# Two attention blocks on one core: stack loads, x and weight pieces asked for at other places, the first maxima later, small VectorE work given more steps, and a new order of the main loop

## The chip, the cores and the metric

One core of a Trainium2 chip. The metric is the device time of one launch in microseconds (us), the median of several runs; lower is better. The engines are TensorE (PE, with its weight loads as PEld), VectorE (DVE), ScalarE (ACT), GpSimd (POOL) and SyncE (SP), which here issues nearly all DMAs, one after the other.

## The reference

Two independent attention blocks, A and B, each with its own x of 2048 rows by 640 columns, its own `wqkv` (640 x 1920) and `wo` (640 x 640), all float32, 32 heads of 20 columns:

```
qkv = x @ wqkv                        # q, k, v per head, Dh = 20, scale = Dh ** -0.5
A:  idx    = s - 2 * (0 .. 7)         # window of 8 keys, every second row back, masked below 0
    logits = sum_d q[s, d] * k[idx, d] * scale
    o      = softmax(logits over the 8) @ v[idx]
B:  scores = q @ k.T * scale          # all 2048 keys
    o      = softmax(scores) @ v
out = concat(A: o @ wo, B: o @ wo)    # 2048 x 1280
```

## The kernel before

Every float32 product is made exact enough by splitting an operand into a high and a low half (`split`: ScalarE casts the high half, VectorE or POOL subtracts to get the low half) and three passes over the pairs (`PASSES`). The output of a split is ready only when its raw piece has landed and both have run; `wait[0]` says how many ticks after the request these two are put into their engines' queues. A tick is one step of the program's own calendar (`tick`, `after(n, fn)`); it sets the order in which instructions are written, and each engine executes its own in that order.

The work comes in stages:

- q and k of A, 128 rows at a time, stored to DRAM (`qa_d`, `ka_d`). From there POOL computes A's whole attention in 16 tiles of 128 rows: each tile has 8 units (4 for scores, 4 for values), whose keys or values are fetched as rows (`akv`), multiplied and added in halves. `a_work` is a generator that writes POOL's next piece; `a_pace(us)` lets it write as much as POOL's own clock `gp.us` allows. A's softmax (`a_softmax`) has two small VectorE jobs per tile: a maximum (`am<-al`) and a reciprocal, put on a list (`soft_jobs`) with the number of steps until they are written.
- q and k of B: ten weight tiles (`w`), in five pairs `m = 0, 2 .. 8`, each with four column groups `n` and two weights `j`, so 8 groups a pair. The result is cast and its low half subtracted (`pr`), and stored to DRAM (`qb_d`, `kb_d`).
- v of A and then of B, in 15 "blocks" of four groups (`v_group`, `v_matmuls`; the sixteenth is finished later): block = 2 x (quarter of x) + half of the columns. x (`xn`, `xl`, loaded by `x_load`) and the weights (`ww`, loaded by `wide_pieces`, for B's v by `w_load`) come in pieces. POOL makes the low halves of x here, VectorE those of the weights. In each tick of most blocks `v_tick` also writes one step of B's maxima pass (`b_max`).
- B's main loop of 512 steps. B's heads are held in 8 "stacks" of four heads; a stack has k (`bk`), four chunks of q (`bq`) and v (`vb`), loaded by `b_pieces` and `v_piece` from DRAM. Each score is computed twice: once with the query rows as output rows for the maxima (VectorE, `mx<-ps_st`), which run `LEAD` = 52 steps ahead, and once with the keys as output rows for the exponentials (ScalarE, `e<-ps_st`) and the product with v (`b_pv`). Output parts are copied by ScalarE (`more`) and added by POOL (`braw<-braw,more`); `more` has four buffers, one taken every two steps. When a chunk is done, `normalize` sends its sums through DRAM (`s_d`), takes a reciprocal on VectorE (`sm<-sm`) and multiplies on POOL.
- In the main loop A's finished tiles are also turned: `a_turn` transposes in five parts on VectorE (`turn<-ao`) into a buffer of tag `stg` (three buffers, shared with `wo_a`'s pieces, loaded in `begin` from `loads` and split by POOL), sends them through DRAM and reads them back (`back`). Then TensorE multiplies them by `wo_a` (`out_chunk`).
- The last steps of B's loop and its output product.

The order of the main loop is written out in the string `ORDER`: `V` ends a step (product with v, and `begin` with its loads and jobs), `S` is two halves of scores with exponentials, `M` and `N` two halves of maxima, `Y` one of each, `j` a part of a turn, `H` a part of A's output product; the digits are PSUM banks. It was made by a planner outside of the kernel; the kernel only reads it.

All DMAs of SP stand in one queue order. The DMA semaphores go round over eight places, so a DMA is issued only when the one eight places before it has landed.

In the listing the functions print as they were. In the profile almost all instructions have line 70 (71 after the change), that of the helper which issues them, so tiles are told apart by their names.

Of the kernel before, what the change touches and what calls it, by code (L numbers as in the profile page):

```python
# [74 lines left out]
def attention_pair(ctx, tc, xa, wqk_a, wv_a, wo_a, xb, wqk_b, wv_b, wo_b, oa, ob):  # L75
# [327 lines left out]
    def a_attention():  # L403
# [3 lines left out]
        for n, (t, c) in enumerate(UNITS):  # L407
# [3 lines left out]
            run_jobs(soft_jobs, 2)  # L411
# [335 lines left out]
    def b_pv(i):  # L747
# [159 lines left out]
    def v_tick(us, maxima=True):  # L907
# [4 lines left out]
        if q_loads:  # L912
            for _ in range(4):
                q_loads.pop(0)()
# [11 lines left out]
    def w_load(half):  # L926

        WV[1][half], pieces = wide_pieces(wv_b[half])
        wait[0] = 2
# [3 lines left out]
    x_load(1, 5)  # L933
    for block in range(15):
        c, half = divmod(block, 2)
        s0 = c % 4 * 4
        if block in (0, 14):
            for s in range(s0, s0 + 4):
                v_group(c, half, s)
                v_tick(2.2, False)  # L940
        else:
            ps4 = [bank() for _ in range(4)]
            for second in range(2):
                for u in range(2):
# [5 lines left out]
                    v_tick(V_US)  # L950
        if half:
            if c < 6:
                x_load(c + 2, 3)
# [4 lines left out]
        if block in (6, 7):  # L958
            w_load(block - 6)
# [28 lines left out]
    def begin(i):  # L988

        g, sub = divmod(i, NQC * NKB)  # L990
        if sub == (1 if g else 2) and g + 1 < NG:
            k_loads, q_loads = b_pieces(g + 1) if g else ([], q1_loads)
            for n, fn in enumerate(k_loads + q_loads + [lambda g=g + 1: v_piece(g, 0, NKB)]):
                after(1 + (n // 2 if n < 8 else 2 * n - 12), fn)
# [3 lines left out]
        if loads and i % 2:  # L998
# [5 lines left out]
        if done_a and done_a[0][0] <= 0 and len(turned) + len(turn_jobs) < 2:  # L1004
# [13 lines left out]
        "Y07M1S36Y54V0Y71S26M4Y03V7Y06M4S31Y72V0Y13M4S76VY71M2S64Y05V7Y64S31N02VY06S15M3Y27V6Y01M3S52VY70M1S53Y46V0Y75"  # L1018
        "M1S34VjS73jM5S42Y10jV7jM5S43Y02VS16M4S30Y27jV1Y36M4S07VY26S03M4Y71V6S02jM4Y37VY02S13M4S76Y02jV1jS75jM3Y26VY07"
        "Y53M1S46Y70V3Y45M1jS67VY04M5S71Y23V0Y17M5S42VY71M3S25S06N17V2Y03S14M5VY70M3S15S26Y07V1M3S27Y65VM3S07Y25V6jY01j"  # L1020
        "S73jH54jH54S02H54Y71H54Y03H54M1VjY70M4S31Y26V0Y73M4S12VY71H62N35S04H62Y71H62Y03H62Y54H62M0Y73V5Y46M0S72VS74M2"
        "S60N15V7S64M2Y01VM5S04Y32V7Y01M5S43VY04H32Y15Y76H32Y40H32Y15H32Y47H32M0S65V4Y73S62M0VY73S26M0V5Y74S32M0VN74S36"
        "H01Y25H01Y73H01Y46Y25H01H01M3Y76V2M0S73Y45VY07S16M3V5Y70S12M3VY07S61M3V2Y07S65M3VY07M5S41H32H32Y70H32Y14Y56H32"
        "Y70H32S14M5V7Y03S21Y64VM2S01Y45V6Y70M2S15VY70S15M2Y46V0Y71M2S54VY71M4S63Y20V1Y76S53N42VS07N63H45M1H45S06H45Y73"
        "H45H45M1S06Y73V4Y50M1S36VY07S35M1Y64V7Y03S21N56VY05M2S14Y67V5Y01S42N36VY70S14M2Y65V0Y71M2S46VjS71jM4S63Y20V7j"
        "M4S61Y30VY61S25Y43jN07jS61V2Y03S45N67VY06M3S51Y72V6Y50M3S17VY05S71M3S26N50V7Y14M2S65VY06M4S13Y72Y60V1Y75M3S26V"
        "Y07M5Y24S31Y70V2Y13M5S74VY70M3S15S26N70V1S25M3Y76VY02S73M4S61N02V7S63M4Y01VY62S03S45N17V6S03M1Y74VY05H12Y73H12"
        "Y64Y05H12Y37H12Y64H12Y03Y75V6Y41M2S05VY70S15Y42N36V7S05N12S34VN06S51Y23V4Y05M6S13VY05S13M6Y24V5Y01S67N32VY06M3"
        "S71H25H25Y06H25Y71Y34H25Y06H25Y71N34V0S17S62N35VM3S71Y56V2jY70M3S16VjY70S15M3S62jY07V1jM3S56Y72VM3S05Y26V7S01"
        "S35jN64VM0S26Y34V5Y70M1S64VS07Y63S42N15V0Y73S16N45VY71M2S46S50N17V4Y35M1S06VY07M5S31S42N70V3Y41M5S72VY70M1S46"  # L1030
        "S35N07V4Y36M1S05VY07M5S31S42N70V3S41M5Y72VY04M5S71Y23V0Y17S64Y52VY71Y62H34H34Y50H34Y72Y61H34Y05H34S72N61V0Y36"
        "S75N14VY71M2S65Y40V1Y76M2S54VY07M5S42Y31V7Y04S65M2VS06M4S13Y27V0M4S16Y73VY12H65Y74H65Y03H65Y41Y72H65Y03H65Y41"
        "N72V0S13M5Y74VY31S72Y65N04V3S72Y15Y06VjM4S72Y61V0jS75jM3Y12VY75M3S61S20jY75jV6M3S21Y05VM3Y72S15V0Y74S16M2VY71"
        "S64M2Y50V1S76M2Y45VY07S62M3S51N07V6S52M3Y01VY75S04M2S16V7Y05M2S14VY06S51M2S47N06V5S41M2Y07VY64S03M1S75N64V0S71"
        "M2Y65VY71S62M3S50N71V6S52M3Y70VY51Y72H34Y06H34S51H34Y27H34Y05H34M6S21V0Y35M6S42VY15S24M6Y30V5Y12M6S43VY04M1S37"
        "Y65V4Y03M1S76VY07M5S31Y24V7Y03M5S12VY04M1S35Y67V4Y03S52N16VS70Y15H23N46H23S75H23Y40H23Y17H23M5S04N71V2S03M5S74"
        "VM0S73Y65V4jY70M1S35VjY07S63Y52Y14jV7jM2S06Y45jVM2S01Y65V4Y70M2S51VY07S16M2S54N70V1Y23M5S74VS07M2S46N51V0S72M3"
        "Y56VY71S25M3S60N71V2S36M4Y70VY13S74M5S02N13V7S06M4Y12VY06S15M3S27N06V1S25M3Y07VS26S05M3Y71V2Y03S46N15VY70M3H16"
        "S25H16Y07H16Y24Y53H16H16N70S24Y53V1Y02M6S34VS02M3S75Y61V0M3S72Y15VM3S72Y56V1Y07M3S26VY07S62Y35Y41V7M5S02Y13VM5"
        "S04Y32V1Y07M5S24VY07Y23H45Y61H45S07M2H45Y61H45Y07H45M2S61V0Y74S56Y13VM4S73Y62V1jY07S54M2VS07jM5S42Y31V0jM5S74"  # L1040
        "Y21VN73S46S52Y10Y74jV3jM5S40Y21VM5S70Y41V2Y37M5S01VS70M3S15Y62V7M3S01Y25VM3S06Y51V2Y07M3S16VY70M5S41S32N07V4"
        "Y35S06M1VY07M5S31S42N70V3Y41M5S72VY70M1S46S35N07V4Y36M1S05VY07M5S31S42V7Y03S61M4VS06Y32H14N57H14S02H14Y56H14"
        "Y07H14M2Y56V7Y04M2S15VS06M4S13Y27V0M4S16Y73VM4S61Y23V7Y06S15M3VY06M1S35Y47V6Y03M1S54VY70S53M1H46H46Y70H46Y53"
        "Y21H46Y70H46M2S51V7Y06S54M2VY06S15M2Y47V6Y01M2S54VjS70jM4S13Y26V7jY01M4S63VM0S26Y54jV3jY70M1S46VY07S64M1S35N70"
        "V6Y14S32Y75VY01M3S25V7Y60M1S34VY06S53M1S47N60V5Y41M2S67VY04M6S13S25N40V1Y27S63M4VY07M2S64S51N70V6Y52M3S71VY70"
        "M1S53S46N07V5Y41M2S06VY70S61M2S45N07V6S41Y23N05VY74S03H21N56H21S74H21Y05H21Y37H21M4S06V7Y13S02M4VY06S13M4Y27V6"
        "M0S53Y42VM0S75Y43V2Y75M0S64VY73M5S40Y12V7Y03M5S41VM3S02H15Y67H15Y04Y23H15Y67H15Y04H15M2S76V0Y15S74M2VY71S64M2"
        "S50V1Y76M2S45VjY07S64M2V5jY70S61M2VjY07S61M2S45jY70jV6M2S41Y05VY74M2S15V0Y74S16M2VY71S64Y53M0S72Y63V4Y57S01M2V"
# [3 lines left out]
        "S75Y46V1jY07M2S56VjY07M5S42S31jY70V4Y35S62M0VY73S65M0V2Y73S46M0VY73S46M0Y52V7Y63M0S45VY62M3S50S71Y26M3S05Y76V1"
        "Y02S34M5VY07S23M5Y41V7Y02M5S34VS03M1S46Y57V0Y14M2S76VY15S74M2V6Y50S71M2VY70S15M2Y46V0Y71M2S54VN71S64H52Y03H52"
        "S67H52Y41H52Y30H52N71Y64V0Y75S16M2VY71M4S63Y20V1Y76M4S32VY07M2S64Y51V7Y06M2S45VY06M4S13Y27V6Y01M4S32VY70Y13H24"
        "Y56H24S70N13H24S56H24Y71H24N03Y56V1Y07S24N35VY07S62M3Y51V7S06jM3S25VjM0S26Y34V5jS70jM1Y64VY70M1S36Y45jV0S76M1"
# [121 lines left out]
```

## Time and profile before

| what | value |
|---|---|
| median of 3 runs | 1779.23 us (1778.9 to 1779.62) |
| profiled execution | 1781.89 us, of which the span is 1780.1 |
| mean granted TensorE clock | 0.988 of full speed |
| busy in the span, TensorE | 1734.6 us, 97% |
| VectorE, ScalarE, POOL busy | 1358.2, 1340.4, 1265.4 us |
| TensorE idle for VectorE's maxima (`mx`) | 24.1 us in 12 waits, longest 8.7 |
| TensorE idle for `bq` from DRAM | 11.3 us in 2 waits, longest 11.0 |

How to read it: times run from the start of the span. TensorE is busy nearly throughout, and the other engines work beside it, so the stretches in which it stands still are few, and the timeline shows each with its start and the instruction that released it. q and k of A end at about 147 us, q and k of B at about 283, the v stage at about 470, A's work on POOL at about 1410. Shares of busy time are averages over these stages. The clock has to be read by windows: it is 1.0 in most of them.

### The profile page before, as it was taken

What the parts mean: (1) busy time and instruction counts of PE and PEld (TensorE: products, weight loads), DVE (VectorE), ACT (ScalarE), POOL (GpSimd) and SP (SyncE); (2) the same over time, 40 slices, a digit from 0 to 9 for tenths busy, and PEclk for the clock granted to TensorE, in tenths of its full rate; (3) what the DMA queues carried; (4) which work ended last, traced back from release to release, by engine and by line L of the source; (5) the groups of instructions that cost most, each with busy time, mean ns of one, the idle gap of its engine ahead of it and who ended that gap; (6) DMA issues with size and microseconds to landing.
All of it is one profiled execution on the core that took longest, in us unless ns stands there. A gap on an engine that the chain in (4) does not pass through costs nothing. (4 is left out here: it accounts for less than half of the span.)

```text
span 1780.1 us, 34705 instructions
## 1 busy us (share of the span) xinstructions
PE 1734.6 (97%) x12711; PEld 1014.8 (57%) x12711; DVE 1358.2 (76%) x1814; ACT 1340.4 (75%) x2658; POOL 1265.4 (71%) x1119
## 2 busy tenths in 40 slices
PE   9999997989979999999999999999999999999999
PEld 8988876989735544444444444344434455444569
DVE  3113332888679999999999999899989999999400
ACT  4223222222479999999999999899989999999981
POOL 0001941698889999999999999999998943545242
PEclk9999998999999999999999999999999999999999
DMA  6447868565764345335436533643552432111123
GB/s 221 122 148 256 273 216 257 194 224 174 218 172 128 99 128 165 114 116 159 131 101 176 148 104 107 186 122 102 167 156 85 115 102 52 40 32 55 33 70 114
DMA packets 194435, 248.29 MB, mean 139 GB/s; under 512 B 89308, under 2 KB 114396, under 8 KB 193272
## 3 DMA queue, kind: packets, MB, share of 16 engines
q1 hardware_dynamic: 193688, 245.41, 45.7%
q8 instruction: 100, 1.64, 0.4%
q14 instruction: 71, 0.58, 0.1%
q10 hardware_dynamic: 576, 0.66, 0.1%
HBM read 181.08 MB, written 64.91 MB: 138 GB/s over the span
## 5 line engine op out<-in xcount | busy, mean ns | idle before, releaser
L70 DVE TENSOR_REDUCE mx<-ps_st 128x1 f32<-128x512 f32 (+1 forms) x1490 | 1226.5, 881 | 74.6 <-PE ps_st L70 63.2
L70 ACT ACTIVATE e<-ps_st 128x512 f32<-128x512 f32 x2048 | 1066.5, 626 | 49.4 <-PE ps_st L70 35.4
L70 PE MATMUL ps_st<-bk,bq 60*128 60x512 f32 x2048 | 563.4, 439 | 31.1 <-DVE mx L70 19.2
L70 PE MATMUL ps_st<-e,vb 128*32 128x512 f32 x4096 | 546.6, 608 | 5.7 <-DVE mx L70 4.9
L70 PE MATMUL ps_st<-bq,bk 62*128 62x512 f32 x2048 | 549.9, 433 | 0.9 <-ACT e L70 0.6
L70 PEld LDWEIGHTS ps_st<-bq,bk 62*128 62x128 f32 x2048 | 274.6, 185 | 407.8 <-ACT e L70 260.1
L70 POOL TENSOR_TENSOR braw<-braw,more 128x512 f32<-128x512 f32 x224 | 288.1, 1286 | 108.3 <-ACT more L70 107.8
L70 PEld LDWEIGHTS ps_st<-bk,bq 60*128 60x128 f32 x2048 | 258.9, 185 | 128.9 <-DVE mx L70 72.8
L70 POOL TENSOR_TENSOR akv<-akv,aq 128x1280 f32<-128x1280 f32 x64 | 188.5, 2945 | 166.7 <-DMA akv<-ka_d 166.7
L70 POOL TENSOR_TENSOR akv<-akv 128x640 f32<-128x640 f32 (+3 forms) x304 | 283.4, 932 | 15.0
L70 ACT COPY ro<-ps_st 128x320 f32<-128x320 f32 (+2 forms) x172 | 73.6, 465 | 176.9 <-PE ps_st L70 112.1
L70 PE MATMUL ps_st<-ww,xn 64*128 64x320 f32 (+1 forms) x1776 | 189.9, 313 | 0.8 <-DVE ww L70 0.6
L70 PEld LDWEIGHTS ps_st<-ww,xn 64*128 64x128 f32 (+1 forms) x1776 | 178.3, 190 | 16.3 <-ACT e L70 8.3
L70 PEld LDWEIGHTS ps_st<-e,vb 128*32 128x32 f32 x4096 | 82.3, 108 | 155.6 <-issue 76.1
L70 POOL TENSOR_TENSOR akv<-akv,al 128x1280 f32<-128x1280 f32 x64 | 151.5, 2367 | 0.6 <-ACT e L70 0.6
L70 ACT COPY more<-ps_st 128x512 f32<-128x512 f32 x224 | 135.7, 606 | 5.3 <-PE ps_st L70 4.6
L70 PE MATMUL ps_st<-xn,w 128*128 128x512 f32 x480 | 116.4, 390 | 1.9 <-DVE w L70 1.9
L70 POOL TENSOR_TENSOR xn<-stg,xn 128x512 fp32r<-128x512 f32 (+1 forms) x30 | 53.8, 1805 | 81.8 <-ACT xn L70 80.5
L70 PEld LDWEIGHTS ps_st<-xn,w 128*128 128x128 f32 x480 | 90.0, 188 | 22.0 <-DVE w L70 2.8
L70 PE MATMUL ps_st<-ww,aot 64*128 64x320 f32 x960 | 100.3, 308 | 0.0
L70 PEld LDWEIGHTS ps_st<-ww,aot 64*128 64x128 f32 x960 | 91.7, 186 | 4.9 <-issue 0.7
L70 ACT CAST pr<-ps_st 128x512 fp32r<-128x512 f32 x40 | 23.5, 586 | 93.4 <-PE ps_st L70 90.5
(65 smaller groups left out, 1045.2 us busy)
## 6 DMA issues: line engine op xcount, KB each, us to landing
akv<-ka_d SPq DMA_DIRECT2D x128, 320.0 KB
akv<-va_d SPq DMA_DIRECT2D x128, 320.0 KB
kb_d<-pr SPq DMA_DIRECT2D x20, 512.0 KB
qb_d<-pr SPq DMA_DIRECT2D x20, 512.0 KB
bk<-kb_d SPq DMA_DIRECT2D x16, 640.0 KB
bq<-qb_d SPq DMA_DIRECT2D x64, 160.0 KB
stg<-xb SPq DMA_DIRECT2D x16, 512.0 KB
rb<-s_d SPq DMA_DIRECT2D x128, 64.0 KB
```

Of the source, the lines that this page charges most:

```text
L70: return self.tc.keep_in_program_order(op(*a, **k))
```

## The change

Eight edits and a new `ORDER`:

- While B's q and k are made, A's pace on POOL is reckoned with groups that are 0.91 as long (`A_SLOW`).
- In the last pair (`m == 8`) the stack of heads 0 to 3 is asked for from the third to the sixth group, its first chunk of q after the seventh, x of the first quarter after the second; the first weights of v in the seventh group of the pair before; the second weights after the last group.
- x of the second quarter is asked for after the second group of the first block, not ahead of it; x of later quarters is split at the fourth tick after its request, not the third.
- The first two blocks have no maxima; they start with the third. The queries of stack 0 are then asked for two DMAs a tick instead of four.
- The weights of B's v are asked for after block 4 (split nine ticks later) and within block 7 (split four ticks later), instead of after blocks 6 and 7 (two ticks later).
- A's small softmax jobs have 5 steps instead of 3, with one more piece of POOL's calendar behind each; the general run of two jobs ahead of each unit goes.
- The reciprocal of B's sums is taken 8 steps after the sums were sent instead of 6.
- In the main loop, loads of the next stack come one a step, `wo_a`'s pieces one in each of the first steps, and turning starts only when no `wo_a` piece is left and after step 10.

```diff
+A_SLOW = 0.91
...
-        job(soft_jobs, 3, lambda: dve.tensor_reduce(m[:, 0], L.rearrange("p o h -> p h o"), AX.X, ALU.max))
+        job(soft_jobs, 5, lambda: dve.tensor_reduce(m[:, 0], L.rearrange("p o h -> p h o"), AX.X, ALU.max))
         yield
+        yield
+        run_jobs(soft_jobs, 9)
...
-        job(soft_jobs, 3, lambda: dve.reciprocal(m[:, 0], m[:, 0]))
+        job(soft_jobs, 5, lambda: dve.reciprocal(m[:, 0], m[:, 0]))
         yield
+        yield
+        run_jobs(soft_jobs, 9)
...
             a_fetch(n + 2)
-            run_jobs(soft_jobs, 2)
...
-                elif m == 8 and (n, j) == (0, 1):
+                elif m == 6 and (n, j) == (3, 0):
                     w0, loads = wide_pieces(wv_a[0])
-                elif m == 8 and n == 3:
-                    if j == 0:
-                        wait[0] = 4
+                elif m == 8:
+                    g8 = 2 * n + j
+                    if g8 == 1:
+                        k_loads, q_loads = b_pieces(0)
+                        wait[0] = 5
+                        XV = [x_pieces(xa, 0)]
+                        for fn in XV[0][1]:
+                            fn()
+                    elif 1 < g8 < 6:
+                        k_loads.pop(0)()
+                    elif g8 == 6:
+                        for _ in range(4):
+                            q_loads.pop(0)()
+                    elif g8 == 7:
+                        wait[0] = 3
                         w1, more = wide_pieces(wv_a[1])
                         for fn in more:
                             fn()
-                if m == 8 and (n, j) == (1, 1):
-                    wait[0] = 3
-                    XV = [x_pieces(xa, 0)]
-                    for fn in XV[0][1]:
-                        fn()
-                    wait[0] = 2
-                if m == 8 and n > 1:
-                    if (n, j) == (2, 0):
-                        k_loads, q_loads = b_pieces(0)
-                    k_loads.pop(0)()
...
-                    a_pace(QK_US * groups)
+                    a_pace(A_SLOW * QK_US * groups)
...
-            normalize(raws.pop(u), g, qc * 512, *((2, 3) if last else (5, 6)), (lambda: out_last(qc)) if last else None)
+            normalize(raws.pop(u), g, qc * 512, *((2, 3) if last else (5, 8)), (lambda: out_last(qc)) if last else None)
...
-        if q_loads:
-            for _ in range(4):
-                q_loads.pop(0)()
+        for _ in range(min(2, len(q_loads))):
+            q_loads.pop(0)()
...
-    x_load(1, 5)
...
-        if block in (0, 14):
+        if block < 2:
             for s in range(s0, s0 + 4):
                 v_group(c, half, s)
                 v_tick(2.2, False)
+                if (block, s) == (0, 1):
+                    x_load(1, 5)
...
+                if block == 7 and not second and u:
+                    w_load(1, 4)
+        if block == 4:
+            w_load(0, 9)
         if half:
             if c < 6:
-                x_load(c + 2, 3)
+                x_load(c + 2, 4)
...
-        if block in (6, 7):
-            w_load(block - 6)
...
-                after(1 + (n // 2 if n < 8 else 2 * n - 12), fn)
+                after(1 + (n if n < 8 else 2 * n - 7), fn)
...
-        if loads and i % 2:
+        if loads and (i % 2 or i < 12):
             loads.pop(0)()
...
-        if done_a and done_a[0][0] <= 0 and len(turned) + len(turn_jobs) < 2:
+        if done_a and done_a[0][0] <= 0 and len(turned) + len(turn_jobs) < 2 and not loads and i > 10:
             a_turn(*done_a.pop(0)[1:])
...
-        "Y07M1S36Y54V0Y71S26M4Y03V7Y06M4S31Y72V0Y13M4S76VY71M2S64Y05V7Y64S31N02VY06S15M3Y27V6Y01M3S52VY70M1S53Y46V0Y75"
...
+        "Y07S61M2Y45V0Y71S26M3Y05V7Y06M3S52Y71V0Y26M3S75VY71M5S24S03N17V2Y06S15Y34VM0S74Y56V3Y70S21N46VY70M4S12S63N07V1"
...
```

How the edits move instructions is seen in each engine's own order. First VectorE in the third and fourth pair of B's q and k, before: `w` is the low half of a weight tile, `pr` that of a result, `am<-al` the maximum of one tile of A.

```order
L70 TENSOR_TENSOR w<-stg,w 128x640
L70 TENSOR_REDUCE am<-al 128x32
L70 TENSOR_TENSOR pr<-ps_st,pr 128x512
L70 TENSOR_TENSOR w<-stg,w 128x640
L70 TENSOR_TENSOR pr<-ps_st,pr 128x512 x7
```

The same place now:

```order
L71 TENSOR_TENSOR w<-stg,w 128x640
L71 TENSOR_TENSOR pr<-ps_st,pr 128x512
L71 TENSOR_TENSOR w<-stg,w 128x640
L71 TENSOR_REDUCE am<-al 128x32
L71 TENSOR_TENSOR pr<-ps_st,pr 128x512 x7
```

The maximum has moved from ahead of the second weight's low half to behind it.

SP at the end of B's q and k and the start of the v stage, before (`wv_a` weights of A's v, `bk` and `bq` keys and queries of stack 0, `xa` x of A, `va_d` rows of v):

```order
L70 DMA stg<-wv_a 128x640 x2
L70 DMA stg<-wv_a 128x320
L70 DMA bk<-kb_d 40x4096
L70 DMA qb_d<-pr 128x2x512
L70 DMA bk<-kb_d 22x4096
L70 DMA stg<-xa 128x2x512 x2
L70 DMA stg<-xa 128x512
L70 DMA va_d<-ro 128x320
L70 DMA bq<-qb_d 20x1024
L70 DMA bq<-qb_d 40x1024
```

And now, from the third piece of k on:

```order
L71 DMA bk<-kb_d 40x4096
L71 DMA qb_d<-pr 128x2x512
L71 DMA bk<-kb_d 22x4096
L71 DMA qb_d<-pr 128x2x512
L71 DMA bq<-qb_d 20x1024
L71 DMA bq<-qb_d 40x1024
L71 DMA bq<-qb_d 20x1024
L71 DMA bq<-qb_d 40x1024
L71 DMA qb_d<-pr 128x2x512
L71 DMA stg<-wv_a 128x640 x2
L71 DMA stg<-wv_a 128x320
L71 DMA va_d<-ro 128x320
```

k and the first queries of stack 0 have moved ahead of the last store of q, and the second weights of v, which stood ahead of the last pieces of k, now stand behind all of them.

VectorE in the first steps of the main loop, before (`turn<-ao` are parts of a turn, `mx<-ps_st` maxima of scores):

```order
L70 STREAM_TRANSPOSE turn<-ao 128x128 x2
L70 TENSOR_REDUCE mx_4423<-ps_st 128x2
L70 TENSOR_REDUCE mx_4423<-ps_st 128x1
L70 STREAM_TRANSPOSE turn<-ao 128x128 x2
L70 TENSOR_REDUCE mx_4423<-ps_st 128x2
L70 TENSOR_REDUCE mx_4423<-ps_st 128x1
L70 TENSOR_REDUCE am<-al 128x32
```

And now:

```order
L71 TENSOR_REDUCE mx_2158<-mx_4500 128x16
L71 STREAM_TRANSPOSE mtr<-mx_2158 128x32
L71 TENSOR_REDUCE mx_5061<-ps_st 128x2
L71 TENSOR_REDUCE mx_5061<-ps_st 128x1
L71 STREAM_TRANSPOSE turn<-ao 128x128 x2
L71 TENSOR_REDUCE mx_5061<-ps_st 128x2
L71 TENSOR_REDUCE mx_5061<-ps_st 128x1
```

The first turn has moved from ahead of the end of a set of maxima (`mx_2158<-mx_4500` gathers it) to behind it.

More of the change, by code (lines that the diff above doesn't have):

```diff
@@ L924, in x_load, with w_load @@
             fn()
-    def w_load(half):
+    def w_load(half, w):
         WV[1][half], pieces = wide_pieces(wv_b[half])
-        wait[0] = 2
+        wait[0] = w
         for fn in pieces:
             fn()
-    x_load(1, 5)
     for block in range(15):
@@ L1022, in attention_pair @@
[L1022 to L1036, printed above, removed]
@@ L1052, in attention_pair @@
[L1052 to L1055, printed above, removed]
-        "Y34VY75S61M2Y40V7Y61S25M3VY06M1S53S74Y60M1S35Y70V4Y36M1S05VY07S63M1Y54V7Y60S13N25VY06S14M2Y57V6Y01M2S45VY70M4"
@@ new lines, in attention_pair @@
+        "Y06H35M1Y74V0Y35M1S76VY73M4S62Y10V3Y76M4S21VY07M1S64Y53V7S60M1Y45VY06Y14H32Y75H32Y06H32Y14H32Y07H32M5Y41V0S72"
+        "M3Y56VY71S25M3Y60V7Y15M3S62VY06M1S53Y74V6S50N13Y27VY05Y41H23Y76H23Y05H23Y41H23Y07H23M4S61V0VY71M4S63H20H20Y17"
+        "H20Y36Y54H20Y17H20M5Y34V1S07M2Y65VY07S62M3Y51V0Y72S63M4VY71M2S64Y05V1Y74S26N30VN72S36H54Y01H54Y73H54Y62Y01H54"
+        "H54M6Y32V0Y15M6S43VY15M3S27Y06V5Y12S74N30VY76S41M2Y05V6Y74M2S10VY75H01Y24H01Y35Y76H01Y24H01Y35H01M6Y24V3S05M1"
+        "S76VjM4S70Y12V6jY75M3S02VY70S15M3S26jY07V1jM3S25Y76VjM3S02Y56V7Y04S31N26VY05S14M2Y67V5Y01S42N36VY70S14S32N65"
@@ new lines, in attention_pair @@
+        "jY46V7S05S12M3VM5Y01S43V2Y07M5S14VY70M3H56S21H56Y70H56N24S31H56Y70H56M2Y14V7S06Y51N23VS04M5S12Y73V0Y16M4S32V"
+        "Y71S63M4V2Y70S16M4VY70Y16H54M2H54S70H54Y61H54H54M2S07N16V5S04M2Y71VS04M6Y32V1Y04M6S53VY02M4S37Y61V2Y03S74M5V"
+        "Y70M3S15H62H62Y70H62N15S34H62Y70H62Y13N45V7S60M2Y14VS05M2S16Y74V0Y15M2S46VY71S54M2V6Y70S51M2VY70S15M2Y46V0Y71"
+        "M2S54VY71M4H63S02H63Y71H63N04S52H63Y71H63N05Y24V7S60M2S15VY06S14M2V5Y06S71M2VY07S64M2S15N70V6Y14M2S75VY70M4S13"
+        "S26N07V1Y25M3S06VY07Y62S53Y41N70V6S51S23N74VM0S72Y54V3Y07S61N24VY07M5S12Y43V7Y01S62N54VY06S51M2S47N60V5Y41M2"
@@ L1078, in attention_pair @@
+        "Y07M5S31S42N70V3Y41M5S72VY70M1S46S35N07V4Y36M1S05VY07M5S31S42N70V3Y41M5S72VY70M1M5S43S70")
     owed = []
```

87 lines of the change are left out of this document (48 added, 39 removed).

## The prediction

> **What bounds the kernel now.** I read the page's busy shares first, then TensorE's (PE's) waits, then the timeline at each long wait, then the clock around it. Busy shares and span:
>
> ```profile
> span 1780.1 us, 34705 instructions
> PE 1734.6 (97%) x12711; PEld 1014.8 (57%) x12711; DVE 1358.2 (76%) x1814; ACT 1340.4 (75%) x2658; POOL 1265.4 (71%) x1119
> ```
>
> TensorE is idle for 1780.1 - 1734.6 = 45.5 us. The change leaves the arithmetic as it is, so it can act only on that idle time and on what idling costs in clock. Who ends TensorE's waits (us in total, times, longest):
>
> ```profile
> PE ps_st L70 <- DVE mx L70: 24.1, 12, 8.7
> PE ps_st L70 <- DMA bq<-qb_d: 11.3, 2, 11.0
> PE ps_st L70 <- DVE w L70: 1.9, 2, 1.4
> ...
> PE ps_st L70 <- DVE ww L70: 0.6, 2, 0.3
> ```
>
> So 38 of the 45.5 us sit in a few places. The timeline of TensorE (start, duration, instruction, in brackets the idle time before it and its releaser) has them:
>
> ```profile
> 232.20 2.58 PE L70 MATMUL ps_st<-xn,w 128*128 128x512 f32 x10 [1.38 <-DVE w L70]
> 306.98 0.76 PE L70 MATMUL ps_st<-bk,bq 60*128 60x512 f32 x1 [11.00 <-DMA bq<-qb_d]
> 387.41 0.79 PE L70 MATMUL ps_st<-bk,bq 60*128 60x512 f32 x2 [4.32 <-DVE mx L70]
> 506.99 0.80 PE L70 MATMUL ps_st<-bk,bq 60*128 60x512 f32 x2 [8.71 <-DVE mx L70]
> 827.52 1.06 PE L70 MATMUL ps_st<-e,vb 128*32 128x512 f32 x8 [0.85 <-DVE mx L70]
> 1132.13 1.93 PE L70 MATMUL ps_st<-e,vb 128*32 128x512 f32 x8 [3.90 <-DVE mx L70]
> 1330.60 1.22 PE L70 MATMUL ps_st<-bk,bq 60*128 60x512 f32 x3 [3.42 <-DVE mx L70]
> ```
>
> Behind each of the five waits of 3.42 us or more the windows show the granted clock at half (the number ahead of the DMA share), and none behind 0.85:
>
> ```profile
> 298.70:312.00 13.30, 4.75 (x29) 4.24 (x31) 2.36 (x2) 2.71 (x3) 8.11 (x5) 0.50 0.67 223
> 387.50:394.20 6.70, 6.36 (x40) 5.58 (x42) 3.65 (x4) 0.00 (x0) 6.31 (x7) 0.50 0.92 304
> 503.60:510.30 6.70, 3.31 (x14) 1.03 (x14) 4.84 (x9) 1.57 (x3) 6.25 (x6) 0.51 0.50 153
> 827.00:833.00 6.00, 5.47 (x40) 2.12 (x42) 5.93 (x8) 5.04 (x11) 6.00 (x6) 1.00 0.61 172
> 1131.70:1138.30 6.60, 6.17 (x26) 2.00 (x28) 4.41 (x8) 2.20 (x5) 6.60 (x5) 0.50 1.00 300
> 1329.70:1336.30 6.60, 5.70 (x23) 2.06 (x27) 4.53 (x6) 3.10 (x6) 6.52 (x5) 0.50 0.61 202
> ```
>
> Work done at half clock takes twice as long, so each long wait costs half of its window's PE time more: 2.4, 3.2, 1.7, 3.1 and 2.9 us. That is an upper bound, as some of that time is not bound by the clock.
>
> **The change part by part.** VectorE's (DVE's) side of the stalls, and the POOL and SP rows that matter:
>
> ```profile
> 199.55 0.63 DVE L70 TENSOR_REDUCE am<-al 128x32 f32<-128x256 f32 x1 [4.58 <-POOL al L70]
> 200.70 2.42 DVE L70 TENSOR_TENSOR w<-stg,w 128x640 fp32r<-128x640 f32 x1
> 380.24 5.98 DVE L70 TENSOR_TENSOR ww<-stg,ww 128x640 fp32r<-128x640 f32 x3
> 398.98 1.95 DVE L70 TENSOR_TENSOR ww<-stg,ww 128x640 fp32r<-128x640 f32 x3
> 505.31 0.51 DVE L70 STREAM_TRANSPOSE turn<-ao 128x128 f32<-128x128 f32 x2 [8.87 <-POOL ww L70]
> 1131.28 0.25 DVE L70 RECIPROCAL sm<-sm 128x16 f32<-128x16 f32 x1 [3.85 <-DMA sm<-s_d]
> 1328.82 0.59 DVE L70 TENSOR_REDUCE am<-al 128x32 f32<-128x256 f32 x1 [3.92 <-POOL al L70]
> ...
> 281.70 3.53 SPq L70 DMA_DIRECT2D stg<-wv_a  x3
> 293.90 7.97 SPq L70 DMA_DIRECT2D bq<-qb_d  x4
> 342.20 1.45 SPq L70 DMA_DIRECT2D stg<-xa  x3
> 363.67 2.43 SPq L70 DMA_DIRECT2D stg<-xb  x3
> ...
> 291.61 0.73 ACT L70 CAST ww<-stg 128x640 fp32r<-128x640 f32 x1 [3.39 <-DMA stg<-wv_a]
> 292.39 0.56 PE L70 MATMUL ps_st<-ww,xn 64*128 64x320 f32 x4 [0.23 <-ACT ww L70]
> 302.77 1.04 ACT L70 CAST xn<-stg 128x1024 fp32r<-128x1024 f32 x1 [7.80 <-DMA stg<-xa]
> 303.89 4.65 POOL L70 TENSOR_TENSOR xn<-stg,xn 128x1024 fp32r<-128x1024 f32 x2 [59.91 <-ACT xn L70]
> 356.01 1.29 POOL L70 TENSOR_TENSOR xl<-stg,xl 128x512 fp32r<-128x512 f32 x1
> 400.91 2.38 POOL L70 TENSOR_TENSOR xn<-stg,xn 128x1024 fp32r<-128x1024 f32 x1 [2.75 <-ACT xn L70]
> ```
>
> *Slower pacing of A in the q/k stage (A_SLOW).* At 199.55 the softmax maximum of A stands in VectorE's row ahead of the low half of a weight (200.70) and holds it for 4.58 us. The order of the changed kernel has it behind that low half. The two waits on `w`, 1.9 us, shrink to what the 2.42 us low half costs by itself: 0.7 left, gain 1.2. What of A's work is not done here comes later on POOL, which idles in the v stage (59.91 us ahead of 303.89): nothing.
>
> *Stack 0 and the first maxima.* Now 11.00 idle, 2.4 of clock and 0.6 on `ww`: 14.0. The four bq issues take 7.97 us because the queue is full of large bk transfers. In the new order bk and the first bq are asked for some groups earlier, and the maxima start at the third block, so the 11.00 goes. Two things are late next. First, the weights of v's second block are asked for behind them, after the last q store. Their first cast came 291.61 - 281.70 = 9.9 us after the first issue, and TensorE needed them about 292. Asked for at 286 to 290 (four groups of bk in front) they are there between 290 and 299: a stall of 0 to 8, I take 5, plus 2 of clock (1.7 to 3.2 after the others). Second, x of the second quarter: its casts now stand behind the block's second copy, so they begin one group before its use. Cast 1.04 and low halves 4.65 and about 1.3 end 7 after they begin, 3.4 beyond what a group and the queue behind it hide. New cost 5 + 2 + 3.4 = 10.4, gain 3.6 (bounds: none of it late 14.0; both at their worst and the clock twice, 8 + 3.2 + 3.4 + 2.4 = 17, a loss of 3).
>
> *The weights of B's v.* The three low halves at 380.24 take 5.98 us while POOL is busy for 6.31 of the window's 6.70; the same three at 398.98 take 1.95, where POOL has 2.75 us idle just after. VectorE's maxima are late by 5.98, TensorE feels 4.32 plus 3.2 of clock, 7.5. The change moves both sets by some blocks, but takes nothing out. One set of two stays beside POOL work: gain 0. Bounds: no set, gain 7.5; both, loss 7.5. A page's rule is heavier: the Trainium skill, "SBUF — State Buffer", section "Who interferes with whom", has a VectorE instruction with two SBUF inputs and a reading GpSimd one exclude each other for a whole instruction. The 5.98 against 1.95 agrees; by it alone both sets pay when POOL never pauses there.
>
> *Turning of A, with wo_a's loads.* At 505.31 VectorE stands 8.87 us before `turn`, whose buffer is held by wo_a pieces that wait for POOL's split. The change asks for wo_a one piece a step for twelve steps and starts turning only when none is left. Gain 8.71 + 1.7 = 10.4. Behind it on SP, the first queries of stack 1 now queue among wo_a pieces; their need is later, 0, at most 2.
>
> *Reciprocal of B's sums, 6 to 8 steps.* The wait of 3.85 at 1131.28 is shorter than two steps (2.4 us each by the kernel's own rhythm). Gain 0.85 + 3.90 + 3.1 = 7.85.
>
> *A's small jobs, 3 to 5 steps.* The last tile's 3.92 at 1328.82 would fit in two steps if POOL were no later than now. That is not sure (below); half of 3.42 + 2.9 = 6.3: 3.15.
>
> *x pieces split at the fourth tick, not the third.* A tick is 2.72 us of v work by the kernel's own rhythm. The tightest low half now ends at 356.01 + 1.29 = 357.3, 6.4 before the next request at 363.67, where its use begins: about 3.7 left. I put 2 for it (0 to 5), since ACT and POOL carry other work there.
>
> *POOL's lag.* ScalarE (ACT) copies a part of an output, POOL adds it later, here behind one of A's multiplications:
>
> ```profile
> 1119.08 0.69 ACT L70 COPY more<-ps_st 128x512 f32<-128x512 f32 x1
> 1131.21 2.36 POOL L70 TENSOR_TENSOR akv<-akv,al 128x1280 f32<-128x1280 f32 x1
> 1133.53 1.27 POOL L70 TENSOR_TENSOR braw<-braw,more 128x512 f32<-128x512 f32 x1
> ```
>
> The addition begins 14.45 us after the copy. Four buffers, one used every two steps, hold 4 x 4.8 = 19.2. Stalls that go are time in which POOL caught up, so the lag grows: cost 2 (0 to 8).
>
> *Sum.* 1.2 + 3.6 + 0 + 10.4 + 7.85 + 3.15 - 2 - 2 = 22.2. The profiled execution took 1781.89, 1.79 around its span, and is 2.66 above the median of 1779.23. So 1781.89 - 22.2 = 1759.7, and as a median **1757**. Its own range is 1748 to 1766 (the open terms with half of their bounds).
>
> **The rivals.** 0.2% is 3.6 us, about what a measurement of this kernel can tell from no change.
>
> 1. *The open terms all fall well:* the weights in time, x still 3.4 late, low halves of B's weights beside an idle POOL, the last tile's wait gone, nothing for x and lag. Gains 1.2 + 10.6 + 7.5 + 10.4 + 7.85 + 6.3 = 43.9; 1781.89 - 43.9 - 2.66 = 1735. For it: every named wait has an edit. Against: each stall is also POOL's pause. 0.15.
> 2. *Both sets of low halves beside POOL work.* The sum loses 7.5: 1764.5. For it: POOL busy 6.31 of 6.70 there. Against: it did pause at 400.91. This is where the skill's "SBUF — State Buffer" rule, section "Who interferes with whom", leads if POOL does not pause. 0.13.
> 3. *The first stall is handed on whole,* to the weights of v and x: the gain of 3.6 turns into -3, and the change does not do there what it says: 1763.6. 0.07.
> 4. *POOL becomes the bound of the loop.* The lag of 14.45 reaches 19.2, ScalarE's copy waits, and what the reciprocal and the small jobs gain (11.0) is paid back there: 1768, or 1775 together with rival 2. 0.11.
> 5. *Slower: x pieces come late in the v stage.* Place: the six requests for x from the third quarter on. If POOL has three of A's multiplications (2.36 each by the row at 1131.21) ahead of the low halves, the 3.7 us of slack is gone and each request stalls TensorE by some 3.4, which brings half clock: 6.3 each, as at 1330.60. The gain of 22.2 is gone from the fourth on; with six, 38 us: 1757 - 2 + 38 = 1793. For it: 2.7 of at most 6.4 us of slack are given away. Against: 6.4 was the tightest of those read, and POOL idled 2.75 before one of them. 0.09.
>
> The forecast's own case keeps 0.45.
>
> **How the numbers follow.** The forecast, rivals 2 and 3 and nearly all of 1 and 4 are faster by over 3.6 us; with parts of 5 (fewer than four late) and of 4: faster 0.83, same 0.05, slower 0.12. The range takes in most of rival 1 and rivals 2 to 4: 1738 to 1777, with about a tenth left out at each end.
>
> **What would show it.** In the changed kernel: no wait on `bq<-qb_d`; no VectorE idle before `turn` or `sm`; TensorE waits on `ww` near 292 to 300 and on `xn` or `xl` before the third block; one long set of `ww` low halves with a wait of some 4 us. Wrong would be: waits on `xn` or `xl` from 340 to 470 (rival 5); a POOL lag near 19.2 with waits on POOL in ScalarE's row (rival 4); half clock at places without a row above.

## The result and the profile after

| | before | after |
|---|---|---|
| median | 1779.07 us (1778.52 to 1779.62, 4 runs) | 1761.97 us (1761.88 to 1764.22, 4 runs) |
| profiled execution, span | 1781.89, 1780.1 | 1762.02, 1760.2 |
| mean granted clock | 0.988 | 0.991 |

The ratio is 0.9907, 95% interval 0.989 to 0.9924: 13.5 to 19.6 us faster. The profiled executions differ by 19.9. Page of the changed kernel, span and busy shares:

```profile
span 1760.2 us, 34683 instructions
PE 1734.1 (99%) x12711; PEld 1014.8 (58%) x12711; DVE 1357.8 (77%) x1816; ACT 1338.2 (76%) x2658; POOL 1265.9 (72%) x1119
```

The engines are busy for nearly as long as before (ScalarE 2.2 us less). TensorE's idle time went from 45.5 to 26.1 us, which is 19.4 of the 19.9. Its waits now (total, times, longest):

```profile
PE ps_st L71 <- DVE mx L71: 10.7, 7, 4.6
PE ps_st L71 <- ACT ww L71: 4.8, 1, 4.8
PE ps_st L71 <- POOL xn L71: 2.6, 2, 1.4
PE ps_st L71 <- ACT e L71: 1.6, 3, 0.8
PE ps_st L71 <- POOL ident L71: 1.4, 1, 1.4
```

The long waits of before on `bq` (11.0) and at the first turn (8.7) are gone, and so is the one on the reciprocal. The timeline of TensorE shows what is left:

```profile
294.65 3.90 PE L71 MATMUL ps_st<-ww,xn 128*128 128x320 f32 x12 [4.83 <-ACT ww L71]
307.90 1.14 PE L71 MATMUL ps_st<-ww,xn 64*128 64x320 f32 x12 [1.42 <-POOL xn L71]
310.22 1.70 PE L71 MATMUL ps_st<-ww,xn 64*128 64x320 f32 x10 [1.18 <-POOL xn L71]
377.09 0.80 PE L71 MATMUL ps_st<-bk,bq 60*128 60x512 f32 x2 [4.64 <-DVE mx L71]
395.42 0.80 PE L71 MATMUL ps_st<-bk,bq 60*128 60x512 f32 x2 [2.22 <-DVE mx L71]
1312.29 0.50 PE L71 MATMUL ps_st<-bk,bq 60*128 60x512 f32 x2 [2.69 <-DVE mx L71]
1642.05 0.49 PE L71 MATMUL ps_st<-bq,bk 62*128 62x512 f32 x1 [0.78 <-ACT e L71]
1643.03 1.20 PE L71 MATMUL ps_st<-bq,bk 62*128 62x512 f32 x7 [0.49 <-ACT e L71]
```

How much each stretch gave is read from marks: the start of the same copy on ScalarE in both timelines. `braw` n is the copy that begins output chunk n (32 in all, counted from 0), one about every 38 us. The idle time is the window's length less TensorE's busy time in it.

| up to | before | after | shift | of this stretch | change of TensorE's idle time in it | forecast |
|---|---|---|---|---|---|---|
| last pair of B's q and k | 259.46 | 257.12 | -2.3 | -2.3 | -2.0 | -1.2 |
| v rows of the third block | 326.37 | 318.48 | -7.9 | -5.6 | -4.7 | -3.6 |
| `braw` 0, start of the loop | 483.43 | 480.52 | -2.9 | +5.0 | +1.8 | 0, and +2 for x |
| `braw` 2 | 568.70 | 554.07 | -14.6 | -11.7 | -9.2 | -10.4 |
| `braw` 16 | 1102.89 | 1089.29 | -13.6 | +1.0 | -0.3 | -0.85, and +2 for the lag |
| `braw` 18 | 1185.09 | 1165.42 | -19.7 | -6.1 | -4.6 | -7.0 |
| `braw` 30 | 1651.69 | 1629.87 | -21.8 | -2.1 | -1.1 | -3.15 |
| end of the span | 1780.1 | 1760.2 | -19.9 | +1.9 | +0.6 | 0 |

Two of these marks do not stand behind the same work. Matmuls of the maxima (tile `bk`) ahead of the third block's rows, before and after (the number behind the length is TensorE's busy time, with the count):

```profile
259.46:326.37 66.91, 5.88 (x28) 3.26 (x28) 0.90 0.74 235
257.12:318.48 61.36, 1.88 (x12) 1.24 (x12) 0.92 0.78 258
```

The sixteen that are missing are four steps of maxima, which now stand behind the mark. A group of v takes 2.2 us in the trace and 2.7 with such a step, so an estimated 2 of the -5.6 and of the +5.0 are work that has moved, and about -3.6 and +3 are left. In the same way, A's output product (tile `aot`) ahead of `braw` 2:

```profile
483.43:568.70 85.27, 6.29 (x60) 5.77 (x60) 4.57 (x4) 0.96 0.57 156
480.52:554.07 73.55, 3.38 (x30) 3.23 (x30) 2.28 (x2) 1.00 0.56 166
```

Thirty of these matmuls follow behind the mark now. TensorE's busy time fell by 2.5 us in this stretch, so some 2 to 3 of the -11.7 are not gained there, and the +1.0 of the next stretch is a small gain.

What remains of the +5.0 ahead of the loop, about 3 us, is the low halves of B's v weights: 1.8 of idle time, and about 7 us more at half clock (the granted clock was 0.96 in the stretch, and 0.98 before). VectorE and POOL there, one instruction a row where they differ:

```profile
369.60 0.81 DVE L71 TENSOR_TENSOR ww<-stg,ww 128x640 fp32r<-128x640 f32 x1
370.33 3.02 DVE L71 TENSOR_TENSOR ww<-stg,ww 128x640 fp32r<-128x640 f32 x1
373.28 2.62 DVE L71 TENSOR_TENSOR ww<-stg,ww 128x320 fp32r<-128x320 f32 x1
390.36 2.73 DVE L71 TENSOR_TENSOR ww<-stg,ww 128x640 fp32r<-128x640 f32 x1
393.01 1.21 DVE L71 TENSOR_TENSOR ww<-stg,ww 128x640 fp32r<-128x640 f32 x2
...
369.66 5.90 POOL L71 TENSOR_TENSOR xn<-stg,xn 128x1024 fp32r<-128x1024 f32 x2
389.45 2.95 POOL L71 TENSOR_TENSOR akv<-akv,aq 128x1280 f32<-128x1280 f32 x1
```

The first set now meets the low halves of x, the second one of A's multiplications. The first instruction of the second set takes 2.73, and ends 0.7 after POOL's at 392.40; its two followers, beside an idle POOL, take 1.21 together. In the first set 0.81 (begun 0.06 ahead of POOL's) is followed by 3.02 and 2.62, and POOL's two take 5.90 (4.69 at 305.48, beside an idle VectorE). Each waits for the other's whole instruction. That is what the Trainium skill says ("SBUF — State Buffer", section "Who interferes with whom"), and the trace agrees.

### The profile page after: what moved, and what is told of

It is laid out like the page before. It is cut to its first block, busy times and chain, and to the rows that moved or that the text cites. A ratio compares the mean times of both kernels' runs of the same rounds, so it can differ in the third digit from the quotient of the medians.

```text
span 1760.2 us, 34683 instructions
## 1 busy us (share of the span) xinstructions
PE 1734.1 (99%) x12711; PEld 1014.8 (58%) x12711; DVE 1357.8 (77%) x1816; ACT 1338.2 (76%) x2658; POOL 1265.9 (72%) x1119
## 3 DMA queue, kind: packets, MB, share of 16 engines
q8 instruction: 100, 1.64, 0.4%
## 4 chain that ended last, share of the span: by engine, by line
PE 77%; POOL 13%; DVE 5%; DMA 2%; ACT 2%; issue 2%; POOLq 0%; SPq 0%; DVEq 0%; ACTq 0%
PE ps_st L71 77%; POOL akv L71 7%; DVE mx L71 4%; POOL braw L71 3%; ACT e L71 1%; POOL ao L71 1%; DMA qb_d<-pr 1%; DVE ww L71 1%; POOL aot L71 1%; POOL al L71 0%; POOL ro L71 0%; DMA stg<-wv_a 0%; DMA stg<-xa 0%; DMA tr_d<-turn 0%; ACT more L71 0%
```

## The experiments

Times are the span of the profiled execution (1780.1 before, 1760.2 after) and the median (1779.07 and 1761.97); the ratio is to runs of the kernel before in the same session, whose medians were 1778.9 to 1780.0. A span is one execution. The executions of one kernel differ by 1 to 6 us. In seven of the kernels the program is the same up to 294 us, and still the wait on `ww` there was between 4.3 and 6.7. So a difference of 2 or 3 us between two spans says little unless its place is known.

| run | span | median | ratio to before, 95% interval |
|---|---|---|---|
| e1_turn | 1764.9 | 1768.39 | 0.9928 to 0.9961 |
| e2_gap6 | 1762.7 | 1763.93 | 0.9901 to 0.9931 |
| e3_soft3 | 1762.4 | 1766.15 | 0.9917 to 0.9946 |
| e4_order | 1778.0 | 1782.81 | 1.0007 to 1.0026 |
| e5_wv | 1758.5 | 1760.46 | 0.9878 to 0.9907 |
| e7_wpool | 1782.9 | 1786.43 | 1.003 to 1.0066 |
| e9_turn_only | 1778.5 | 1782.58 | 1.0007 to 1.0026 |
| e10_order_only | 1777.9 | 1779.05 | 0.9985 to 1.0004 |
| e11_uncounted | 1755.8 | 1758.53 | 0.9862 to 0.9892 |
| e12_front | 1757.1 | 1757.63 | 0.9857 to 0.9886 |
| e13_both | 1753.8 | 1755.17 | 0.984 to 0.9873 |
| e14_old_pair | 1772.1 | 1776.38 | 0.9969 to 0.9988 |

### One part undone in the changed kernel

**e1_turn**, turning and wo_a's loads as before:

```diff
-        if loads and (i % 2 or i < 12):
+        if loads and i % 2:
...
-        if done_a and done_a[0][0] <= 0 and len(turned) + len(turn_jobs) < 2 and not loads and i > 10:
+        if done_a and done_a[0][0] <= 0 and len(turned) + len(turn_jobs) < 2:
```

> The changed kernel with the turning and wo_a's loads as before (turning not held back, wo_a's pieces asked for in every second step), all else new. My theory: the stall before the first turn comes back, 8.7 us idle and some 3 more in half clock and catching up, so 10 to 12 us slower than the changed kernel (its profile 1762.0, so about 1773). Rival (the new order by itself moved the turn behind the end of wo_a's pieces): within 2 us of the changed kernel.

The stall did not come back: VectorE waits 0.64 us ahead of the first turn part, as the new order has its `j` later anyway. The loss came in pieces: 1.8 up to `braw` 0, before the edit acts (the wait on `ww` was 6.32), 1.5 at the turn, 3.4 around two waits of 1.26 and 1.20 for the turned tile at 584, some 3.3 over the loop with no wait of its own; the last tile's wait is gone in return, 4.2, some 0.6 are lost after it, and 1.6 come back at the end, where half clock did not occur. In all 4.7 in span and 6.4 in the median. My theory fell here, and the rival's bound too.

**e2_gap6**, `(5, 8)` back to `(5, 6)` in `normalize`:

> The changed kernel with the reciprocal of B's sums at 6 steps again. My theory: the waits on sm come back where POOL is 14 to 15 us behind ScalarE, and the time grows by 6 to 8 us (about 1769); with the lag of 15.0 at 1134 in the changed kernel rather more than 3.9 us idle there. Rival (the two waits were an accident of the old order): within 2 us.

VectorE's row in this run has the wait again:

```profile
1117.74 0.25 DVE L71 RECIPROCAL sm<-sm 128x16 f32<-128x16 f32 x1 [3.22 <-DMA sm<-s_d]
```

The time there grows by 6.1, and then 3.9 come back: POOL catches up during the stall, and the last tile's wait (2.69 at 1312) is gone in this run. Net 2.5 in span and 2.0 in the median, so my theory fell on the total. The price was right at its place, but part of it is paid back later. I had counted the stalls as independent. (That POOL catches up is argued; what the runs show is the trade. e9_turn_only, below, has it the other way round: its wait at the reciprocal shrank from 3.90 to 0.61, and the last tile's grew from 3.42 to 7.51.)

**e3_soft3**, A's small jobs as before:

> The changed kernel with A's small softmax jobs at 3 steps, without the added pieces of calendar, and with the run of two jobs ahead of each unit, as before. My theory: the last tile's wait of 2.23 on VectorE grows by up to two steps (4.8), other tiles stay without a wait; 1 to 5 us slower (1763 to 1767). Rival (the small jobs wait in several tiles, since POOL lags more than before): three waits or more, over 10 us slower.

The total (2.3 in span, 4.2 in the median) lies in my range by luck. There is no crowd of waits, 0.41 at 735 and 2.92 at 1309, but the last tile's wait on TensorE, which was to grow, is 2.92 for 2.69 in the changed kernel. Instead the loop begins 4.6 earlier, since the second set of low halves costs only 0.51 and 0.63, and 6.5 are lost bit by bit until 1360.

**e4_order**, the old order with all other edits:

> The changed kernel with the old order of the main loop, all other edits new. My theory: the order carries little by itself, since the stalls came from calendar waits, so within 4 us of the changed kernel (1758 to 1766). Rival (the gain sits in the order): over 8 us slower.

The rival held: the whole gain is gone. The marks are level with the changed kernel's up to `braw` 1 (-0.5), and lose 13 us by `braw` 4: 5.9 in waits of at most 1.6, and 7 in which the same matmuls keep TensorE busy for longer, at full clock. Another 5 to 7 go over the rest of the loop. The place of the loss is explained by the program, step by step: the old order has the output products of A's third tile from step 46 on, but with the held-back turning the tile is ready only at step 64. Its first half comes 18 steps late and the second 10, all chunks in one heap. The trace agrees: the copies of this product come at 639 to 641, and at 594 to 614 in e14_old_pair below, where the tile is in time.

### One part alone in the kernel before

**e9_turn_only** takes the turning edit alone, **e10_order_only** the order alone.

> The kernel before with only the turning and wo_a loading edited (turning held back until no piece of wo_a is left and step 10, wo_a one piece a step). After the run of the old order I now hold that turning and order belong together: the stall of 8.71 at 507 goes, but the old order has A's output products at steps for which the turned tile is now late, and 10 to 14 us are lost in the next 120 us; in all within 4 us of before (1778 to 1786 profiled). Rival (holding back is enough by itself): 10 to 12 us faster than before.

> The kernel before with only the new order. My theory: its turn parts stand at later steps, so the stall at 507 goes by the order alone (as it did with the turning edit taken back), 9 to 12 us less there; the waits on sm and on the last tile stay (together 7 us idle, one of them perhaps in place of the other): profile 1768 to 1773. Rival (without the edits the new order misses what it was made for): not faster than before by over 4 us.

ScalarE's copies of A's output products (`ro`) in the window 590 to 660, of e9_turn_only and then of before (three durations in ns, then first and last start):

```profile
L70 ACT COPY ro<-ps_st x4: 425/428/434, 640.9 to 643.4; 128x320 f32<-128x320 f32 x4
```

```profile
L70 ACT COPY ro<-ps_st x4: 426/438/472, 599.2 to 618.9; 128x320 f32<-128x320 f32 x4
```

The four copies come 42 us later with the turning edit and in a heap of 2.5 us, where those of before are spread over 20. The stall of 8.71 is down to 1.34, as expected, and by `braw` 4 all of the gain is lost and 4 more: the turn alone brings nothing. The order alone brought 2.2 in span and 0.7 in the median, where I expected 9 to 14, so the rival's bound held: it wins 7 by `braw` 2, loses that again by `braw` 16 with no wait above 1.6, and at 1133 VectorE still waits 5.66 for `sm`.

**e14_old_pair**: old order and old turning together, all other edits new (e4_order and e1_turn in one).

> The changed kernel with the old order and the old turning and wo_a loading together, all other edits new. No tile is late then. My theory (the old order failed with the new edits only since it met late tiles): the stall of 8 to 9 us near 505 comes back, the loss between 520 and 650 goes, the reciprocal's gain of 6 shows: span 1768 to 1772. Rival (the old order is slower through the whole loop under the new edits): span 1776 or more.

```profile
502.02 0.80 PE L71 MATMUL ps_st<-bk,bq 60*128 60x512 f32 x2 [6.84 <-DVE mx L71]
```

The stall is back, the loss between `braw` 1 and 4 is gone (119.7 us for 132.3 in e4_order), and yet this is 5.9 faster in span than e4_order and 6.4 in the median: late tiles cost more than the stall. Of the 19.9, 8.0 belong to the other edits by the spans, and 12 to turning and order together. But this profiled execution was the fastest of ten; by the medians it is 3.6 and 14. The median lies between my theory and the rival. With the other edits in place the new order alone gives 7.2 (e14_old_pair to e1_turn; 8.0 in the median) and the turning 4.7 more (6.4), 4.6 of them between `braw` 0 and 30; with the old order the turning costs 5.9.

### What is left, taken away

**e5_wv**: DMAs of v's second weights in the fifth group of the last pair, their casts unmoved.

```diff
                     elif 1 < g8 < 6:
+                        if g8 == 4:
+                            raws1 = []
+                            for a, b in PAIRS:
+                                t1 = sb.tile([128, 640], F32, tag="stg", bufs=3, name="stg")
...
+                                sp.dma_start(raw1, wv_a[1][:, a:b])
...
```

> The changed kernel with the DMAs of v's second block of weights asked for three groups earlier (among the pieces of k, into buffers that are free by then); their casts and low halves stay where they are. My theory: TensorE's wait of 4.83 us on ww near 294 goes, with some 2 of clock, the x waits of 2.6 stay, and the lead of 5 to 7 us stays to the end: profile 1755 to 1757. Rival (POOL, which has 2.5 us idle in all from 480 to 1380, sets the end of A and with it of the loop): the lead melts by 1320, within 2 us of the changed kernel's 1762.

The wait on `ww` went, and one on x took its place, 7.22 instead of 4.83:

```profile
305.99 0.64 PE L71 MATMUL ps_st<-ww,xn 64*128 64x320 f32 x2 [7.22 <-ACT xn L71]
```

x was asked for at 294.7, as in the changed kernel (294.9). ScalarE's row shows what holds its cast:

```profile
304.57 0.42 ACT L71 COPY ro<-ps_st 128x320 f32<-128x320 f32 x1 [5.86 <-DMA va_d<-ro]
304.89 1.99 ACT L71 CAST xn<-stg 128x1024 fp32r<-128x1024 f32 x2
```

It stands behind a copy of v's rows whose buffer waits for an earlier store in SP's queue. My expectation missed that. The lead was 3.2 for a moment and +0.5 after that; the 1.7 gained at the end are the half clock near 1642, which did not occur. So the run says nothing on the rival.

**e7_wpool**: low halves of B's v weights on POOL.

```diff
-        WV[1][half], pieces = wide_pieces(wv_b[half])
+        WV[1][half], pieces = wide_pieces(wv_b[half], gp, act.copy)
```

> The changed kernel with the low halves of B's v weights subtracted on POOL instead of VectorE. My theory: the two long sets on VectorE (6.30 and 3.86 us) go, with TensorE's waits of 4.64, 0.34, 2.22 and 0.34 and their clock; 7 to 9 us less at the start of the loop, and as POOL has pauses of 2.6 and 5.3 us in the v stage, 5 to 9 less at the end (1753 to 1757). Rival (POOL sets the end): six more POOL instructions of 0.8 to 1.5, about 7.6 us, come back at the end; 0 to 8 us slower than the changed kernel.

The loop begins 7.6 earlier, as expected, and the end is 22.7 later, far outside both theories. Of the 30.3 lost in between, 25.9 go in four jumps. ScalarE's copies `braw` 7 and 8 in the changed kernel, and the same two in e7_wpool:

```profile
748.82 0.59 ACT L71 COPY braw<-ps_st 128x512 f32<-128x512 f32 x1
786.38 0.58 ACT L71 COPY braw<-ps_st 128x512 f32<-128x512 f32 x1
```

```profile
745.77 0.59 ACT L71 COPY braw<-ps_st 128x512 f32<-128x512 f32 x1
790.16 0.59 ACT L71 COPY braw<-ps_st 128x512 f32<-128x512 f32 x1
```

37.6 against 44.4 us: 6.8 lost. The other three jumps are 6.5, 5.7 and 6.9. In each of them a tile's output products come late. The copies of the fifth tile, changed kernel and e7_wpool:

```profile
L71 ACT COPY ro<-ps_st x4: 425/473/542, 733.2 to 756.9; 128x320 f32<-128x320 f32 x4
```

```profile
L71 ACT COPY ro<-ps_st x4: 425/429/432, 779.2 to 782.7; 128x320 f32<-128x320 f32 x4
```

POOL's own clock `gp.us` counts each `tensor_tensor` that is written, so six more of them move A's units to later steps, and four tiles (the 5th, 7th, 11th and 13th) miss the steps that the order has for them by 16 to 20. What a late tile costs is seen at the 11th. From `braw` 18 to 19 the changed kernel does its 60 matmuls in 40.1 us, and e7_wpool, without them, takes 40.2. From `braw` 19 to 20 the changed kernel has none and takes 36.0, and e7_wpool, with the 60, takes 41.7. The steps that the order has for the products are no shorter without them, and elsewhere the products come on top. Why they are no shorter is not shown.

**e11_uncounted**: the same on POOL, with `gp.us` put back after each, so that every output product keeps its step.

> The low halves of B's v weights on POOL once more, but not counted in POOL's own clock gp.us, by which the program decides how much of A it writes per step. So POOL has the same extra work as in the run before of this kind, and A's output products all fall on their steps (in that run four of the 16 tiles were 16 to 20 steps late). My theory: the loss came from late tiles alone, at 6 to 7 us each; now the 7 to 8 us won at the start of the loop stay to the end: span 1752 to 1755. Rival (POOL, without idle time in the loop, pays for the extra work): the lead of 7 melts by 1320, span 1759 or more.

The same copies in this run:

```profile
745.03 0.59 ACT L71 COPY braw<-ps_st 128x512 f32<-128x512 f32 x1
782.60 0.59 ACT L71 COPY braw<-ps_st 128x512 f32<-128x512 f32 x1
```

37.6 again. The extra work on POOL is the same as in e7_wpool, 8.0 us, and the end is 27 us earlier. The lead of 3.8 at `braw` 0 stays within 0.3 up to `braw` 21. So late tiles do cost 6 to 7 us each. The run does not test what more POOL work inside the loop would cost: the six subtractions fall into POOL's pauses of the v stage, where it is busy for 140.8 of the 150 us from 330 to 480, and for 131.4 in the changed kernel. The lead is half of what I expected: TensorE now waits 1.23 and 1.25 on POOL for `ww`, 0.87 for x, and 1.46 + 0.64 on maxima near 419.

**e12_front**: e5_wv with `x_load(1, 5)` moved ahead of the first block; **e13_both**: e12_front and e11_uncounted.

> The second weights of v asked for earlier, as tried, and x of the second quarter asked for ahead of the first block with its splitting five ticks later. My theory: the two waits are one queue (SP), and with both out of the way the 8.4 us of waits near 294 to 311 fall to 0 to 3, which lasts to the end: span 1752 to 1756. Rival (the wait moves on to the maxima's first queries, or the lead melts): span 1758 or more.

> Both of the edits before together: weights of v and x of the second quarter earlier, low halves of B's v weights on POOL and not counted. My theory: the gains add, 12 to 15 us below the changed kernel's span of 1760.2: 1745 to 1749. Rival (POOL sets the end): 1757 or more.

e12_front fell between its theories: 5.1 ahead from `braw` 0 on, of which 2 go at the last tile; TensorE still waits 4.16 and 1.38 near 303, since x is cast behind a copy that waits for a store in SP's queue:

```profile
301.55 0.43 ACT L71 COPY ro<-ps_st 128x320 f32<-128x320 f32 x1 [11.07 <-DMA va_d<-ro]
301.88 1.99 ACT L71 CAST xn<-stg 128x1024 fp32r<-128x1024 f32 x2
```

e13_both is the fastest of all, 6.4 below the changed kernel in span and 6.8 in the median (interval to before 0.984 to 0.9873), half of the 12 to 15 that I expected; the two gains would add to 7.5 in span (4.4 and 3.1). What it still waits for:

```profile
PE ps_st L71 <- DVE mx L71: 5.6, 6, 2.5
PE ps_st L71 <- ACT xn L71: 4.4, 2, 4.1
PE ps_st L71 <- POOL ww L71: 3.3, 4, 1.3
```

## Why the prediction was right, and where not

The forecast of 1757 was 5 below the measured 1762, in its own range of 1748 to 1766. Measured in the profiled executions, the change gave 19.9 where the sum said 22.2. Sorted by kind, the sum held 15.5 of idle time, with the 4 set aside taken off, and 6.7 of clock. Measured were 19.4 of idle time and 0.5 of TensorE's busy time. The two parts are off by 4 and 6 in opposite directions, so that the total came so near is partly luck. By its steps:

- **Pacing of A.** Both waits on `w` went. 2.3 instead of 1.2: I kept 0.7 for low halves beside POOL, and with the maximum behind them nothing was late. No run takes this edit away alone.
- **First maxima.** 3.6, as the sum said, once the maxima that moved behind the mark are taken off the 5.6. The two waits that I put next are there with nearly the sizes given: 4.83 (5) and 1.42 + 1.18 (3.4).
- **Low halves of B's v weights.** The term that failed: 0 became a loss of about 3. Both sets now lie beside POOL work, 6.30 and 3.86 us, which was rival 2, at less than its price of 7.5. The runs bear the cause out: with the same matmuls, the stretch from the third block to `braw` 0 takes 162.0 us in the changed kernel, 157.5 in e3_soft3, where one set costs little, and 151.7 in e7_wpool, where VectorE has none. One reading was off without changing the argument: the 6.31 us of busy POOL belong to the window behind the first set. Beside that set POOL was busy for 5.74 of 5.98 us, and beside the second for 0.02 of 1.95.
- **Turning.** About 9 for 10.4 when the moved product is taken off the 11.7, with the stall gone as named. But I gave the gain to the turning edit, with the order as bystander. e9_turn_only, e4_order and e14_old_pair show that the edit alone exchanges the stall for late tiles. The prediction came out right since the change brings both.
- **Reciprocal.** 6.1 between `braw` 16 and 18 for 7.0. By e2_gap6 the net worth is 2.0 to 2.5: without it the last tile would wait less.
- **Small jobs.** 2.1 for 3.15. Of the wait more than the half is left, 2.69 of 3.42. And e3_soft3, which undoes this edit, has 2.92 there: the edit hardly acts on the wait that it was priced by, and its 2.3 in span (4.2 in the median) come in small losses elsewhere.
- **x pieces and lag.** 4 were set aside and little was needed: no wait on later x pieces (rival 5 did not occur). With copies and additions matched in order, the lag grew to 15.0 at the copy of 1134 and was 19.5 once, from the copy at 546.89 to its addition at 566.36, which I had named as a sign of rival 4. But that rival needs ScalarE to wait for POOL, and from 480 on it did so for 0.2 us in all; TensorE stood still for 0.8 of the 609 us from `braw` 0 to 16. So rival 4 did not occur. The end instead lost 1.9, below.
- **Clock.** Of the gain, 6.7 was booked as clock. TensorE's busy time fell by only 0.5. At the reciprocal its busy time fell by 1.5 where 3.1 were booked. And half clock came at places that no row had named (310, 395, 1643), which was one of my signs of being wrong: by the mean clock, 2 x 0.012 x 1780 = 43 us of half clock before and 2 x 0.009 x 1760 = 32 after.

Open: the slow losses of 3 to 7 us over the loop in e1_turn, e3_soft3 and e10_order_only, in which no wait stands out. That VectorE's small jobs or turn parts stand at other steps than the order was laid out for would explain them; no run isolates it. Nor does a run undo the pacing, the new places of stack 0, or the later split of x one by one; what they gave is read from the stretches alone.

## What to carry to other kernels

Where the order of one engine is written out and another's work is placed by the program's own clock, the two are one schedule: an edit that takes a stall away, or a few instructions more that this clock counts, can make a tile miss its steps, at 6 to 7 us each here, and cost more than the stall. Write both out and look for work that arrives late, before pricing the edit by its wait. And count a low half with two SBUF inputs on VectorE together with what POOL does at that moment, by the step of the new order and not by the average.

## What the runs showed of the hardware that was not expected

Half clock came without any wait of 3.4 us. In the changed kernel it followed waits of 2.22 at 395 and 2.69 at 1312. Near 1642 the changed kernel and e3_soft3 have the same two short waits (0.78 and 0.49; 0.76 and 0.48), and the clock was halved only in the first. Windows of the changed kernel and of e3_soft3 (the number ahead of the DMA share is the granted clock):

```profile
1641.50:1648.50 7.00, 5.96 (x30) 2.51 (x31) 1.91 (x4) 6.09 (x13) 2.06 (x5) 0.76 0.13 40
```

```profile
1643.60:1650.60 7.00, 5.99 (x41) 3.63 (x42) 1.91 (x4) 5.97 (x13) 2.71 (x5) 1.00 0.13 40
```

From `braw` 30 to 31 the one takes 47.07 us, the other 45.43:

```profile
1629.87 0.61 ACT L71 COPY braw<-ps_st 128x512 f32<-128x512 f32 x1
1676.94 0.66 ACT L71 COPY braw<-ps_st 128x512 f32<-128x512 f32 x1
```

```profile
1631.96 0.61 ACT L71 COPY braw<-ps_st 128x512 f32<-128x512 f32 x1
1677.39 0.66 ACT L71 COPY braw<-ps_st 128x512 f32<-128x512 f32 x1
```

That is 1.64 us for 3.4 us at half clock, and most of the 1.9 lost at the end. It is half of the time at half clock, as the prediction's bound had it. The same two waits came with half clock in e2_gap6, e11_uncounted, e12_front and e13_both (47.0 to 47.1 us for the chunk) and without it in e1_turn, e5_wv and e7_wpool (45.4); what decides it, the runs do not show. Before, a single wait of 0.61 stands there, and no half clock. The price can be less than half: from `braw` 16 to 17, e2_gap6 has the changed kernel's matmuls and takes 6.1 us longer, of which 3.2 are the wait, so 6.8 us at half clock cost 2.85.
